# The output projection of three groups of heads put off to the last group, in a gated attention and MLP kernel

## The chip, the cores and the metric

The kernel runs on one core of a Trainium2 chip. A core has a matrix engine (TensorE, "PE" in the profile, with its weight loads listed apart as "PEld"), a vector engine (VectorE, "DVE"), an activation engine (ScalarE, "ACT"), a general engine (GpSimd, "POOL") and a queue engine that issues transfers (SyncE, "SP"). Each engine takes its instructions in the order of its own queue, and waits for other engines through semaphores. TensorE writes its results to PSUM, which has eight banks of 128 partitions by 512 floats; everything else lies in SBUF or in the chip's main memory.

The metric is the time of one execution on the device in microseconds (us), lower is better. Three runs of the kernel before took 1194.57, 1199.56 and 1199.92 us; the median is 1199.56 us.

## The reference

Everything is computed for 2048 tokens of width 448, in float32:

```python
x = A_x                                        # 2048 x 448
g = sigmoid((x * gate_w).sum(-1))              # one gate per token
q, k, v = split(x @ wqkv)                      # 16 heads of 28
p = softmax(q @ k.T * 28 ** -0.5)              # per head, 2048 x 2048
a = concat_heads(p @ v) @ wo                   # the output projection
y = (x - mean(x)) / sqrt(var(x) + 1e-5)        # layer norm
b = gelu(y @ w1 + b1) @ w2 + b2                # width 1792 inside
out = g * a + (1 - g) * b
```

Products on TensorE are made in a rounded float32 format. To keep the precision, a factor is split into a high and a low part, and a product is three products: high by high, high by low, low by high.

## The kernel before, in words

The tokens are cut into four chunks of 512 (`NC`, `CH`), each of four tiles of 128 tokens (`TPC`). The 16 heads are cut into four groups of four (`NG`); a head takes 32 of the 128 partitions.

**Stage 1, projections of x.** For each chunk `c` seven tiles of q and k (`qk_tile(c, m)`, line 156, eleven products each) and four tiles of v (`v_tile`, line 170) are made. Between them stands the preparation of the layer norm: `ln_stats` (line 189) loads two tiles of x (`bxr`) and takes mean and variance on VectorE; `ln_rows` (line 196) makes the reciprocal deviation; `ln_turn` (line 202) turns means and deviations into rows with two transposes on TensorE (line 207), into two parts of one bank. VectorE copies each result out (line 208) and SP stores it. `ln_load` (line 105) brings the rows back, repeated over all partitions, as `lnr`; `ln_apply` (line 108) loads a tile of x and normalizes it on GpSimd and ScalarE for the MLP. TensorE goes through its instructions in the order of the program text; for the other engines a planner sets the order in this stage and the next.

**Stage 2, the MLP.** Two layers of products (`mlp1`, line 430, and `mlp2`, line 445) for one chunk after the other. The result `b` without its bias goes to main memory (`gbs`). Products for the row maxima of the scores are filled in between (`Filler`, `RowMax`, line 308, each followed by a VectorE maximum, lines 288 and 290).

**Stage 3, attention.** The order of all engines is written out by hand. The loop at line 637 runs over units; a unit is one head's scores of 128 keys by 512 queries, and an iteration takes five units (`U`). There are 205 iterations for four groups by four chunks by 16 key tiles by four heads. In each iteration `scores` (line 587) issues

- up to three products for row maxima (`filler.max.issue`): one into bank 5, later one into bank 6, later one into bank 5 again,
- 15 score products into banks 0 to 4 (line 596), and two exponentials on ScalarE (line 601), one over three banks and one over two;

then `pv_mm` (line 622) adds to the outcome of the chunk in bank 7: eight products in most iterations, sixteen in some (four iterations hold five steps of four products).

When a group and chunk are done, the generator `finish` (line 518) is started, and one of its steps is run behind each of the iterations named in `STEPS` (2, 5, 7, 8, 9, 10 after the end): bank 7 is copied out as `ob`; the sums of the softmax are inverted and spread through main memory (`lt`, `rls`, `rc`); GpSimd scales `ob` and splits it into `oh` and `ol` (lines 534 to 536); and in four further steps `project` (line 508) multiplies one tile of 128 tokens by this group's part of `wo`: three products (lines 511 to 513) into a bank which `take` (line 500) hands out as 6, 5, 6, 5 in turn, and a VectorE operation (line 514) that adds the product times the gate to `acc`. `acc` holds all 16 tiles in SBUF through the whole stage. In group 0 `load_acc` (line 569) fills it with `gbs` for one chunk at step 6, and `gate_acc` (line 572) adds the bias `b2b` and multiplies by one minus the gate, in eight GpSimd instructions for each chunk at step 14. So `project` is called 64 times, 16 times for each group; in the last group the result is stored to `out`. For the very last chunk `finish_last` (line 543) does the same without the way through main memory.

The row maxima of the next chunk are stored by GpSimd's queue (`ms<-mt`, line 278) and loaded by SP at step 12 (`load_qm`, line 411). They are ended at iteration 188.

Of the kernel before, what the change touches and what calls it, by code (L numbers as in the profile page):

```python
# [15 lines left out]
P = 128  # L16
S = 2048
# [22 lines left out]
def kernel(ctx: ExitStack, tc: tile.TileContext, xt, wqk, wv, wo, xk, w1, b1, w2, b2,  # L40
# [43 lines left out]
    def staged(width):  # L84
        return my.tile([P, CH], F32, name="r", bufs=3)[:, :width]
# [19 lines left out]
    def ln_load(c):  # L105
        nc.sync.dma_start(lnr, lns.rearrange("(n t) i -> n (t i)", n=2)[:, c * CH:(c + 1) * CH].partition_broadcast(P))

    def ln_apply(c, t):
        x = staged(CH)
        nc.sync.dma_start(x, xt[t, :, c * CH:(c + 1) * CH])  # L110
        nc.gpsimd.tensor_sub(x, x, lnr[:, 0])
        nc.gpsimd.tensor_mul(x, x, lnr[:, 1])
        nc.scalar.activation(yh[:, t], x, AF.Copy)
        if t < 3:
            nc.gpsimd.tensor_sub(yl[:, t], x, yh[:, t].bitcast(F32))
        else:
            nc.gpsimd.tensor_sub(yh[64:128, t], x[64:128], yh[64:128, t].bitcast(F32))


    with tc.tile_pool(name="qx", bufs=2) as qx, tc.tile_pool(name="qo", bufs=3) as qo, \  # L120
# [93 lines left out]
        for c in range(NC):  # L214
            for m in range(NM):
# [243 lines left out]
    for c in range(NC):  # L459
# [21 lines left out]
        for i in range(TPC):  # L481
            if c + 1 < NC:
                ln_apply(c + 1, i)
            mlp2(c, i)
# [12 lines left out]

    spare = 0

    def take():  # L500

        nonlocal spare
        spare += 1
        return bank[:, 5 + spare % 2]

    acc = aw.tile([P, NT, D], F32, name="acc")
    b2b = aw.tile([P, D], F32, name="b2b")
    def project(g, tt, oh, ol):

        po = take()[:, :D]  # L510
        nc.tensor.matmul(po, oh, woh[:, g], start=True, stop=False)  # L511
        nc.tensor.matmul(po, oh, wol[:, g], start=False, stop=False)  # L512
        nc.tensor.matmul(po, ol, woh[:, g], start=False, stop=True)  # L513
        nc.vector.scalar_tensor_tensor(acc[:, tt], po, gate[:, tt:tt + 1], acc[:, tt], op0=OP.mult, op1=OP.add)  # L514
        if g == NG - 1:
            nc.sync.dma_start(out[tt], acc[:, tt])

    def finish(g, c, pv):
# [12 lines left out]
        yield True  # L531
        oh = ao.tile([P, CH], F32R, name="oh")
        ol = ao.tile([P, CH], F32R, name="ol")
        nc.gpsimd.tensor_mul(ob, ob, rc)
        nc.gpsimd.tensor_copy(oh, ob)
        nc.gpsimd.tensor_sub(ol, ob, oh.bitcast(F32))
        yield True
# [5 lines left out]
    def finish_last(g, c, pv):  # L543

        ob = ao.tile([P, CH], F32, name="ob")
        rc = ao.tile([P, CH], F32, name="rc")
        oh = ao.tile([P, CH], F32R, name="oh")
        ol = ao.tile([P, CH], F32R, name="ol")
        psl = bank[:, 0]
        tiles = [slice(i * P, (i + 1) * P) for i in range(TPC)]  # L550
        for sl in tiles:
            nc.scalar.activation(ob[:, sl], pv[:, sl], AF.Copy)
        for sl in tiles:
            nc.tensor.matmul(psl[:, sl], sel, ob[:, sl], start=True, stop=True)
        for i, sl in enumerate(tiles):
            nc.vector.reciprocal(rc[:, sl], psl[:, sl])
            nc.vector.tensor_mul(ob[:, sl], ob[:, sl], rc[:, sl])
# [11 lines left out]
    def load_acc(c):  # L569
        nc.sync.dma_start(acc[:, c * TPC:(c + 1) * TPC], gbs[c * TPC:(c + 1) * TPC].rearrange("t p d -> p t d"))  # L570

    def gate_acc(c):
        for tt in range(c * TPC, (c + 1) * TPC):
            nc.gpsimd.tensor_add(acc[:, tt], acc[:, tt], b2b)
            nc.gpsimd.tensor_scalar(acc[:, tt], acc[:, tt], ngate[:, tt:tt + 1], None, op0=OP.mult)

# [54 lines left out]
    with tc.manual_schedule(engines={E.SP, E.Pool, E.Activation, E.DVE}):  # L631
# [5 lines left out]
        for u in range(0, 4 * steps, U):  # L637
            units = list(range(u, min(u + U, 4 * steps)))
            while at < units[-1] // 4:
# [3 lines left out]
                if n == 0:  # L643
# [35 lines left out]
        while summed < steps:  # L679
            pv_mm(summed)  # L680
            summed += 1
        finish_last(NG - 1, NC - 1, pv)

# [52 lines left out]
```

## Time and profile before

| | |
|---|---|
| median of three runs | 1199.56 us |
| the profiled execution's own time | 1192.24 us |
| its span from first to last instruction | 1190.5 us |
| mean granted TensorE clock | 0.987 |
| busy: TensorE, VectorE, ScalarE, GpSimd | 95%, 64%, 53%, 28% |
| stage 1 about | 0 to 130 us |
| stage 2 about | 130 to 490 us |
| stage 3 about | 490 to 1190 us |

The views used below: the list of groups of instructions gives for each line, engine and shape the total busy time, the mean in ns, and the idle time of the engine before them with what ended it. The list of waits gives engine and line, what it waited for, the total in us, how often, and the longest. The timeline gives start and duration in us, the engine, the line, the operation, and in brackets the idle time just before. A row of the timeline that ends in x2 stands for two instructions in a row. The stage table gives for each stretch of time the busy time of each engine and the granted TensorE clock as a share of full speed. The chain is the sequence of work that led to the last instruction.

### The profile page before, as it was taken

To read this page: it belongs to the slowest core of one execution; us is meant where nothing else is said; L and a number is where in the kernel's file an instruction comes from. 1 tells how busy PE (TensorE), PEld (TensorE's weight loads), DVE (VectorE), ACT (ScalarE), POOL (GpSimd) and SP (SyncE) were. 2 spreads that over 40 slices of the span, in tenths; PEclk is the share of its full clock that TensorE was granted. 3 is DMA by queue.
4 is the path that set the end of the run, shared out by engine and by line. 5 is a ranking of instruction groups with operands and counts; after the bars stand their busy time and mean duration, and the time that the engine had idled before them with its cause. 6 is when DMAs were issued, how large, how long until landed. Compare 5 with 4: busy or idle time off the path is not lost.

```text
span 1190.5 us, 19884 instructions
## 1 busy us (share of the span) xinstructions
PE 1134.6 (95%) x8136; PEld 679.7 (57%) x8136; DVE 764.2 (64%) x1081; ACT 636.0 (53%) x668; POOL 330.0 (28%) x355
## 2 busy tenths in 40 slices
PE   6989989999999999999999999999999999999997
PEld 5777757777777777644444444444444444444443
DVE  3442198888878888566666666666666666666403
ACT  5333461132131140376767766766766776777774
POOL 4051368045133131136136211301301211220220
PEclk9998999999999999899999999999999999999998
DMA  8886742002101032362200220100210100001101
GB/s 273 255 255 235 210 139 87 16 9 77 39 16 33 17 87 60 102 158 84 58 17 19 57 60 11 35 17 10 66 53 17 28 26 25 11 11 48 34 26 55
DMA packets 53519, 84.35 MB, mean 71 GB/s; under 512 B 8676, under 2 KB 28660, under 8 KB 52628
## 3 DMA queue, kind: packets, MB, share of 16 engines
q1 hardware_dynamic: 49236, 76.96, 21.6%
q0 software_dynamic: 4192, 6.12, 2.2%
q8 instruction: 64, 1.05, 0.4%
q14 instruction: 27, 0.22, 0.1%
HBM read 56.40 MB, written 26.49 MB: 70 GB/s over the span
## 4 chain that ended last, share of the span: by engine, by line
PE 83%; DMA 6%; DVE 4%; POOL 3%; issue 1%; ACT 1%; SPq 0%; DVEq 0%; POOLq 0%; ACTq 0%
PE bank L625 20%; PE bank L596 18%; PE bank L308 14%; PE bank L438 10%; PE bank L450 4%; PE bank L453 4%; PE bank L451 4%; PE bank L163 3%; PE bank L511 2%; DVE acc L514 2%; DMA r<-in_w 2%; DMA xraw<-in_xt 1%; PE bank L179 1%; PE bank L513 1%; PE bank L512 1%
## 5 line engine op out<-in xcount | busy, mean ns | idle before, releaser
L601 ACT ACTIVATE pt<-bank 128x1536 f32<-128x1536 f32 (+1 forms) x410 | 484.6, 1234 | 197.8 <-PE bank L596 193.0
L288 DVE TENSOR_REDUCE mx<-bank 128x1 f32<-128x512 f32 x624 | 412.6, 686 | 145.5 <-PE bank L308 135.3
L625 PE MATMUL bank<-pt,vg 128*32 128x512 f32 x2048 | 262.8, 604 | 0.0
L308 PE MATMUL bank<-khi,qd 28*128 28x512 f32 x512 | 241.8, 478 | 21.7 <-DVE acc L514 20.8
L290 DVE TENSOR_REDUCE mx<-bank 128x2 f32<-128x1024 f32 x200 | 235.2, 1218 | 37.7 <-PE bank L308 37.6
L596 PE MATMUL bank<-qh,klo 28*128 28x512 f32 x1024 | 185.3, 397 | 0.0
L308 PEld LDWEIGHTS bank<-khi,qd 28*128 28x128 f32 x512 | 92.3, 181 | 152.9 <-DVE mx L288 80.1
L596 PE MATMUL bank<-qh,khi 29*128 29x512 f32 x768 | 164.4, 477 | 0.3 <-ACT h L456 0.3
L438 PE MATMUL bank<-y,w1f 128*128 128x512 f32 x616 | 153.1, 399 | 1.1 <-ACT h L442 1.1
L596 PE MATMUL bank<-ql,khi 28*128 28x512 f32 x768 | 136.4, 392 | 0.0
L438 PEld LDWEIGHTS bank<-y,w1f 128*128 128x128 f32 x616 | 112.9, 188 | 37.0 <-issue 12.4
L443 POOL TENSOR_TENSOR hl<-h,hh 128x512 fp32r<-128x512 f32 x56 | 72.2, 1289 | 171.2 <-ACT h L442 160.0
L514 DVE SCALAR_TENSOR_TENSOR acc<-bank,gate,acc 128x448 f32<-128x448 f32 x64 | 43.7, 684 | 105.3 <-PE bank L513 104.1
L596 PEld LDWEIGHTS bank<-qh,klo 28*128 28x128 f32 x1024 | 92.2, 186 | 5.0
L524 POOL DMA_DIRECT2D lt<-ob x15 | 10.8, 720 | 301.6 <-DVE ob L523 301.6
L625 PEld LDWEIGHTS bank<-pt,vg 128*32 128x32 f32 x2048 | 45.7, 108 | 84.2 <-issue 83.0
L308 PE MATMUL bank<-khr,qd 28*128 28x512 f32 x512 | 81.8, 467 | 7.0 <-DVE mx L290 4.7
L453 PE MATMUL bank<-w2h,hl 128*128 128x448 f32 x224 | 84.6, 378 | 0.0
L450 PE MATMUL bank<-w2h,hh 128*128 128x448 f32 x224 | 84.5, 377 | 0.0
L596 PEld LDWEIGHTS bank<-qh,khi 29*128 29x128 f32 x768 | 65.9, 183 | 31.9 <-ACT pt L601 26.4
L456 ACT ACTIVATE h<-bank 128x448 f32<-128x448 f32 x16 | 8.7, 543 | 139.2 <-PE bank L453 139.2
L451 PE MATMUL bank<-w2l,hh 128*128 128x448 f32 x224 | 82.2, 367 | 0.0
(97 smaller groups left out, 1285.3 us busy)
## 6 DMA issues: line engine op xcount, KB each, us to landing
qk<-hl SPq DMA_DIRECT2D x28, 512.0 KB
xraw<-in_xt SPq DMA_DIRECT2D x16, 256.0 KB
vs<-vt SPq DMA_DIRECT2D x16, 256.0 KB
r<-in_xt SPq DMA_DIRECT2D x16, 256.0 KB
rc<-rls POOLq DMA_DIRECT2D x60, 64.0 KB, 2.2
bxr<-in_xk SPq DMA_DIRECT2D x8, 448.0 KB
r<-in_w SPq DMA_DIRECT2D x14, 256.0 KB
gbs<-h SPq DMA_DIRECT2D x16, 224.0 KB
```

Of the source, the lines that this page charges most:

```text
L288: nc.vector.reduce_max(self.mx[:, c0:c0 + 1], bank[:, b0], axis=AX)
L290: nc.vector.reduce_max(self.mx[:, c0:c1 + 1:c1 - c0], bank[:, b0:b1 + 1], axis=AX)
L308: nc.tensor.matmul(bank[:, b], self.qds[self.n][r, i * P:(i + 1) * P], khi[self.n // NC][r, k * 512:(k + 1) * 512], start=True, stop=True)
L438: nc.tensor.matmul(ps, a, b, start=(i == 0), stop=(i == len(ops) - 1))
L443: nc.gpsimd.tensor_sub(hl[f], h, hh[f].bitcast(F32))
L450: nc.tensor.matmul(a, hh[f][:, sl], w2h[f], start=(f == 0), stop=False)
L451: nc.tensor.matmul(a, hh[f][:, sl], w2l[f], start=False, stop=False)
L453: nc.tensor.matmul(a, hl[f][:, sl], w2h[f], start=False, stop=(f == NF - 1))
L514: nc.vector.scalar_tensor_tensor(acc[:, tt], po, gate[:, tt:tt + 1], acc[:, tt], op0=OP.mult, op1=OP.add)
L596: nc.tensor.matmul(bank[:, u % U], a[r, k * P:(k + 1) * P], b[r], start=(i == 0), stop=(i == 2))
L601: nc.scalar.activation(t, bank[:, b:b + len(units)], AF.Exp, scale=SCALE)
L625: nc.tensor.matmul(pv[32 * j:32 * j + 32, :], vg[n // NC][:, k, 32 * j:32 * j + 32], probs.pop(4 * step + j), start=(k == 0), stop=(k == N ...
```

## The change

The change has three parts.

1. **Projection.** `finish` of groups 0 to 2 no longer projects. GpSimd writes the scaled, split outcome into tiles that stay in SBUF (`outcome`, three groups by two parts by 2048 tokens). In the last group each token tile gets one projection of twelve products, three for each group, into one bank, which is always bank 6, and one VectorE operation `gated` in place of four. `finish_last` puts the nine products of groups 0 to 2 of its first tile ahead of the sums of the softmax and those of the other three tiles behind them, in four different banks (1 to 4).
2. **`acc`.** The tile `acc` of 16 token tiles is gone. `load_acc` and `gate_acc` run in the last group (steps 6 and 10) and use the buffers of `vg` and `klo`, which are free by then.
3. **Layer norm preparation.** `ln_apply` is split in two: `ln_fetch` issues the load of x, `ln_apply` computes. In stage 1 the rows of the first four tiles are turned after tile `m` = 5 of chunk 1 (before: 2), and those of the other twelve after tile 4 of chunk 3 (before: tile 5 of chunk 2). `ln_load` moves from tile 3 to tile 6 of chunk 1; the four `ln_apply` calls move from chunks 1 and 2 to chunks 2 and 3.

```diff
+    def ln_fetch(c, t):
+        lnx[c, t] = staged(CH)
+        nc.sync.dma_start(lnx[c, t], xt[t, :, c * CH:(c + 1) * CH])
+
     def ln_apply(c, t):
-        x = staged(CH)
-        nc.sync.dma_start(x, xt[t, :, c * CH:(c + 1) * CH])
+        x = lnx.pop((c, t))
...
-                if c == 1 and m in (0, 2, 3):
-                    (ln_rows if m == 0 else ln_turn if m == 2 else lambda a, b: ln_load(0))(0, TPC)
+                if c == 1 and m == 1:
+                    ln_rows(0, TPC)
+                if c == 1 and m == 5:
+                    ln_turn(0, TPC)
+                if c == 1 and m == 6:
+                    ln_load(0)
...
-                if c == 2 and m in (3, 5):
-                    (ln_rows if m == 3 else ln_turn)(TPC, NT)
-                if c == 1 and m in (4, 6) or c == 2 and m in (0, 2):
-                    ln_apply(0, m // 2 - 2 if c == 1 else m // 2 + 2)
+                if c == 2 and m in (0, 1, 2, 4):
+                    ln_fetch(0, (0, 1, 2, 2, 3)[m])
+                if c == 2 and 3 <= m < 6 or c == 3 and m == 0:
+                    ln_apply(0, m - 3 if c == 2 else 3)
+                if c == 2 and m == 6:
+                    ln_rows(TPC, NT)
+                if c == 3 and m == 4:
+                    ln_turn(TPC, NT)
...
-    def project(g, tt, oh, ol):
-
-        po = take()[:, :D]
-        nc.tensor.matmul(po, oh, woh[:, g], start=True, stop=False)
-        nc.tensor.matmul(po, oh, wol[:, g], start=False, stop=False)
-        nc.tensor.matmul(po, ol, woh[:, g], start=False, stop=True)
-        nc.vector.scalar_tensor_tensor(acc[:, tt], po, gate[:, tt:tt + 1], acc[:, tt], op0=OP.mult, op1=OP.add)
-        if g == NG - 1:
-            nc.sync.dma_start(out[tt], acc[:, tt])
+    outcome = [[aw.tile([P, S], F32R, name=f"o{x}{g}") for x in "hl"] for g in range(NG - 1)]
+    acc = {}
+
+    def project(c, i, oh, ol, po, groups):
+
+        sl = slice(i * P, (i + 1) * P)
+        for g in groups:
+            if g < NG - 1:
+                h, l = (x[:, c * CH:(c + 1) * CH][:, sl] for x in outcome[g])
+            else:
+                h, l = oh[:, sl], ol[:, sl]
+            nc.tensor.matmul(po, h, woh[:, g], start=(g == 0), stop=False)
+            nc.tensor.matmul(po, h, wol[:, g], start=False, stop=False)
+            nc.tensor.matmul(po, l, woh[:, g], start=False, stop=(g == NG - 1))
+
+    def gated(c, i, po):
+        tt = c * TPC + i
+        a = acc[c][:, i]
+        nc.vector.scalar_tensor_tensor(a, po, gate[:, tt:tt + 1], a, op0=OP.mult, op1=OP.add)
+        nc.sync.dma_start(out[tt], a)
...
+        if g < NG - 1:
+            return
         yield True
         for i in range(TPC):
-            sl = slice(i * P, (i + 1) * P)
-            project(g, c * TPC + i, oh[:, sl], ol[:, sl])
+            po = bank[:, 6, :D]
+            project(c, i, oh, ol, po, range(NG))
+            gated(c, i, po)
             yield True
...
+        po = [bank[:, 1 + i, :D] for i in range(TPC)]
         for sl in tiles:
             nc.scalar.activation(ob[:, sl], pv[:, sl], AF.Copy)
+        project(c, 0, oh, ol, po[0], range(NG - 1))
         for sl in tiles:
             nc.tensor.matmul(psl[:, sl], sel, ob[:, sl], start=True, stop=True)
+        for i in range(1, TPC):
+            project(c, i, oh, ol, po[i], range(NG - 1))
...
-        for i, sl in enumerate(tiles):
-            project(g, c * TPC + i, oh[:, sl], ol[:, sl])
+        for i in range(TPC):
+            project(c, i, oh, ol, po[i], [NG - 1])
+            gated(c, i, po[i])
...
-                if g == 0:
+                if g == NG - 1:
                     if k == 6:
                         load_acc(c)
-                    if k == 14:
+                    if k == 10:
                         gate_acc(c)
```

More of the change, by code (lines that the diff above doesn't have):

```diff
@@ L482 @@
             if c + 1 < NC:
+                ln_fetch(c + 1, i)
                 ln_apply(c + 1, i)
@@ L496 @@
     wol = aw.tile([P, NG, D], F32R, name="wol")
[L498 to L506, printed above, removed]
-    b2b = aw.tile([P, D], F32, name="b2b")
-    def project(g, tt, oh, ol):
-        po = take()[:, :D]
[L511 to L514, printed above, removed]
-        if g == NG - 1:
-            nc.sync.dma_start(out[tt], acc[:, tt])
+    b2b = aw.tile([P, D], F32, name="b2b")
+    outcome = [[aw.tile([P, S], F32R, name=f"o{x}{g}") for x in "hl"] for g in range(NG - 1)]
[15 more added lines that the diff above has]
+        nc.sync.dma_start(out[tt], a)
     def finish(g, c, pv):
@@ L531, in finish @@
         yield True
-        oh = ao.tile([P, CH], F32R, name="oh")
-        ol = ao.tile([P, CH], F32R, name="ol")
+        if g < NG - 1:
+            oh, ol = (x[:, c * CH:(c + 1) * CH] for x in outcome[g])
+        else:
+            oh, ol = ao.tile([P, CH], F32R, name="oh", bufs=1), ao.tile([P, CH], F32R, name="ol", bufs=1)
         nc.gpsimd.tensor_mul(ob, ob, rc)
@@ L569, in load_acc @@
     def load_acc(c):
-        nc.sync.dma_start(acc[:, c * TPC:(c + 1) * TPC], gbs[c * TPC:(c + 1) * TPC].rearrange("t p d -> p t d"))
+        a = aq.tile([P, NT, P], F32, name="vg", bufs=2) if c % 2 == 0 else aq.tile([P, S], F32, name="klo", bufs=2)
+        if c % 2 == 0:
+            a = a.rearrange("p a b -> p (a b)")
+        acc[c] = a[:, :TPC * D].rearrange("p (t d) -> p t d", d=D)
+        nc.sync.dma_start(acc[c], gbs[c * TPC:(c + 1) * TPC].rearrange("t p d -> p t d"))
     def gate_acc(c):
-        for tt in range(c * TPC, (c + 1) * TPC):
-            nc.gpsimd.tensor_add(acc[:, tt], acc[:, tt], b2b)
-            nc.gpsimd.tensor_scalar(acc[:, tt], acc[:, tt], ngate[:, tt:tt + 1], None, op0=OP.mult)
+        for i in range(TPC):
+            a, tt = acc[c][:, i], c * TPC + i
+            nc.gpsimd.tensor_add(a, a, b2b)
+            nc.gpsimd.tensor_scalar(a, a, ngate[:, tt:tt + 1], None, op0=OP.mult)
     tc.keep_in_program_order(nc.scalar.activation(gate, zall, AF.Exp, scale=-1.0))
```

10 lines of the change are left out of this document (6 added, 4 removed).

## The prediction, made before the changed kernel ran

> **What bounds the kernel now.** I read the page's sums first, then the list of waits of TensorE by stage, then the timeline of ScalarE in stage 3, whose exponentials mark every iteration. Page:
>
> ```profile
> span 1190.5 us, 19884 instructions
> PE 1134.6 (95%) x8136; PEld 679.7 (57%) x8136; DVE 764.2 (64%) x1081; ACT 636.0 (53%) x668; POOL 330.0 (28%) x355
> ```
>
> TensorE is the bound as a whole, so what counts is its products and its own waits. Its waits in 500 to 1020 us, then in 1020 to 1191 us, then in 0 to 135 us:
>
> ```profile
> PE bank L308 <- DVE acc L514: 17.7, 22, 0.8
> ...
> PE bank L308 <- DVE acc L514: 3.1, 4, 0.8
> ...
> PE bank L207 <- DVE rows L208: 8.3, 2, 5.5
> ```
>
> In attention nearly every idle moment of TensorE is one and the same: the next row maximum product (bank 5) waits until VectorE has read a projection out of bank 5. In stage 1 the second of two transposes waits for VectorE to copy out the first. Timeline of ScalarE, first a finish of group 0, then the last one of group 2:
>
> ```profile
> 588.25 2.37 ACT L601 ACTIVATE pt<-bank 128x1536 f32<-128x1536 f32 x2 [1.20 <-PE bank L596]
> 590.95 2.37 ACT L601 ACTIVATE pt<-bank 128x1536 f32<-128x1536 f32 x2 [0.33 <-PE bank L596]
> 593.66 2.37 ACT L601 ACTIVATE pt<-bank 128x1536 f32<-128x1536 f32 x2 [0.34 <-PE bank L596]
> 596.37 2.37 ACT L601 ACTIVATE pt<-bank 128x1536 f32<-128x1536 f32 x2 [0.34 <-PE bank L596]
> 599.91 2.37 ACT L601 ACTIVATE pt<-bank 128x1536 f32<-128x1536 f32 x2 [1.18 <-PE bank L596]
> 603.42 2.37 ACT L601 ACTIVATE pt<-bank 128x1536 f32<-128x1536 f32 x2 [1.14 <-PE bank L596]
> 608.01 2.37 ACT L601 ACTIVATE pt<-bank 128x1536 f32<-128x1536 f32 x2 [2.23 <-PE bank L596]
> ...
> 617.04 2.37 ACT L601 ACTIVATE pt<-bank 128x1536 f32<-128x1536 f32 x2 [2.89 <-PE bank L596]
> ...
> 1030.73 2.37 ACT L601 ACTIVATE pt<-bank 128x1536 f32<-128x1536 f32 x2 [1.20 <-PE bank L596]
> ...
> 1047.64 2.37 ACT L601 ACTIVATE pt<-bank 128x1536 f32<-128x1536 f32 x2 [2.71 <-PE bank L596]
> ```
>
> Four iterations in a row without a projection (588.25 to 599.91) take 11.66 us: three of 2.71 and one of 3.54, which has sixteen outcome products. The next four, each with one projection of three products, take 17.13 (599.91 to 617.04), and the last four of group 2 take 16.91. So a finish costs 5.47 to 5.25 us, about 5.36. Within it a projection into bank 6 lengthens its iteration by 0.80 (599.91 to 603.42, less 2.71), one into bank 5 by 1.88 (603.42 to 608.01): 1.08 more, for the wait listed above. ScalarE needs 2.37 of the 2.71, so it doesn't hold back an iteration that loses its projection; that iteration falls to 2.71, as its neighbours show.
>
> **Groups 0 to 2: projections removed.** Twelve finishes at 5.36: -64.3 us. Nothing takes their place there: the GpSimd steps that make `oh` and `ol` are the same, only their target is another tile. The 48 VectorE operations that go with them are off the path where they don't hold bank 5.
>
> **Last group: nine more products in each of twelve blocks.** The same form, 448 columns with a new weight for each product, runs in `mlp2`; timeline of TensorE:
>
> ```profile
> 187.78 0.36 PE L450 MATMUL bank<-w2h,hh 128*128 128x448 f32 x1
> ...
> 189.20 0.37 PE L451 MATMUL bank<-w2l,hh 128*128 128x448 f32 x1
> ```
>
> Seven steps in 1.42 us: 0.203 each. 12 x 9 x 0.203 = +21.9 us, all on the path.
>
> **Bank 6 for every projection.** The finish of chunk 12 still runs beside the maxima; its two projections in bank 5 lose their wait: -2.2 us (2 x 1.08); those of chunks 13 and 14 run after or at the end of the maxima and had none. Bound: nothing gained, or every one of the twelve blocks waits as a bank 5 one does now, +13.0. I take the first because the bank 6 blocks of now, with a maximum into bank 6 in the middle of each iteration, show only the 0.80. [...]
>
> **`acc` in the last group.** Eight GpSimd instructions for each chunk move; groups by shape, then GpSimd's and SP's timelines in the last chunk but one:
>
> ```profile
> L575 POOL TENSOR_SCALAR acc<-acc,ngate 128x448 f32<-128x448 f32 x16 | 22.5, 1404 | 1.6
> ...
> L574 POOL TENSOR_TENSOR acc<-acc,b2b 128x448 f32<-128x448 f32 x16 | 18.3, 1142 | 0.0
> ...
> 1113.11 1.28 POOL L536 TENSOR_TENSOR ol<-ob,oh 128x512 fp32r<-128x512 f32 x1
> 1119.56 0.60 POOL L278 DMA_DIRECT2D ms<-mt  x1 [5.17 <-DVE mt L277]
> ...
> 1121.96 0.51 SPq L416 DMA_DIRECT2D qh<-ms  x1
> ...
> 1135.45 2.37 ACT L601 ACTIVATE pt<-bank 128x1536 f32<-128x1536 f32 x2 [0.28 <-PE bank L596]
> ```
>
> Four times 1.404 + 1.142 is 10.2 us for a chunk, while GpSimd otherwise waits. In that chunk they stand ahead of the store of the row maxima (line 278): after `ol`, 1114.4, they end at 1124.6, so the store goes out 5 us later, and SP's load of it (line 416, with the `out` stores that follow it in SP's queue) as much. The scores that need it begin just before 1135.45: 13.5 us of cover today, 8 then. Cost 0; if the cover were gone, at most 5. The loads of `gbs` (four, one for each chunk, as now) go behind SP's `qh` and `ql` loads into buffers whose readers are done a chunk earlier: 0.
>
> **The end.** Timeline of TensorE, ScalarE and VectorE:
>
> ```profile
> 1173.84 2.78 PE L625 MATMUL bank<-pt,vg 128*32 128x512 f32 x24
> 1176.77 0.78 ACT L552 ACTIVATE ob<-bank 128x128 f32<-128x128 f32 x4 [1.71 <-issue]
> 1177.10 1.16 PE L554 MATMUL bank<-ob,sel 128*128 128x128 f32 x8 [0.47 <-ACT ob L552]
> ...
> 1183.20 0.29 DVE L557 TENSOR_TENSOR ob<-ob,rc 128x128 f32<-128x128 f32 x1
> ...
> 1184.75 0.57 PE L512 MATMUL bank<-wol,oh 128*128 128x448 f32 x1
> 1185.12 0.57 PE L513 MATMUL bank<-woh,ol 128*128 128x448 f32 x1
> ...
> 1186.85 0.69 DVE L514 SCALAR_TENSOR_TENSOR acc<-bank,gate,acc 128x448 f32<-128x448 f32 x1 [0.44 <-PE bank L513]
> ```
>
> The outcome products end at 1176.62. Nine products then take 1.83, to 1178.45, and the sums 1.16 more, to 1179.61 (now 1178.26), so VectorE's chain ends 1.35 later, at 1184.84. The other 27 products run beside it, 5.48, to 1185.09; the last twelve take 2.44, to 1187.53; the last VectorE operation 0.69, to 1188.22, against 1187.54 now: +0.7. Today these products go at 0.37 (1184.75 to 1185.12), for a TensorE that had idled; if that stays, 39 x 0.167 = +6.5 more.
>
> **Stage 1.** Products of one stretch, a load, the waiting transposes, what VectorE did ahead of the second copy, and the clock after each wait (chain, timelines, stage table; the seventh figure of a stage row is the granted clock):
>
> ```profile
> 42.88 4.55 DMA bxr<-in_xk
> ...
> 105.28 17.96 PE bank L163 x77
> ...
> 46.60 0.27 PE L207 MATMUL bank<-ident,mr 128*4 128x128 f32 x1
> 49.71 0.27 PE L207 MATMUL bank<-ident,mr 128*4 128x128 f32 x1 [2.83 <-DVE rows L208]
> ...
> 90.05 0.69 DVE L154 TENSOR_TENSOR xh<-xraw,xh 64x512 fp32r<-64x512 f32 x1 [1.08 <-ACT xh L150]
> ...
> 91.38 0.27 DVE L208 COPY rows<-bank 12x128 f32<-12x128 f32 x1
> ...
> 50.90:54.60 3.70, 3.70 (x11) 2.88 (x10) 0.79 (x2) 0.60 (x1) 0.00 (x0) 0.54 0.82 219
> 91.80:95.40 3.60, 3.60 (x10) 2.83 (x10) 0.88 (x2) 1.31 (x3) 2.55 (x2) 0.50 0.92 345
> ```
>
> The second turn waits 5.5 us because VectorE, in its order, first serves the x loads of chunk 3. In the built program it comes in chunk 3, where no x is loaded any more, and only the usual `hl` copy stands ahead: some 0.5 is left (two steps of 0.27), -5.0. The first turn is no better off: ahead of its copy VectorE now has the statistics of a `bxr` tile, whose load SP issues behind the store of tile 2. That tile ends at 46.6. Its store waits for VectorE, which first has the statistics of an earlier `bxr` (landed at 42.88 + 4.55 = 47.4) and two copies of x among six operations; at 0.69 each the store goes out near 52. Another 4.55 for the load, a little for the store ahead of it and two more operations put the copy near 59, an estimate from these rows. TensorE is there after three more tiles of 2.57 (17.96 over seven), at 54.3: some 4.6 of wait in place of 2.83, +1.8. Bounds: 0.5, as for the other, to 8, if two more stores go ahead. The clock cost 3.70 x 0.46 = 1.7 after the first and 1.8 after the second wait; the second goes: -1.8. Together -5.0, bounds -10 to +2. [...]
>
> **Sum.** -64.3 + 21.9 - 2.2 + 0.7 - 5.0 = -48.9 us against the profiled execution's 1192.24: 1143.3. That execution lies 7.3 below the median of the runs, 1199.56; with it the median after is 1150.6, and I predict 1150.
>
> **Rivals.**
> *The single bank waits.* All twelve blocks pay the 1.08 of today's bank 5: +13, 1163. [...] Against: an iteration lies between them, and VectorE needs 684 ns.
> *The layer norm part loses.* The first turn waits 8 or more and the clock gains nothing: 1157.
> *The long blocks are slow.* If twelve products in a row didn't overlap weight loads, each would take both of these (the rows of line 511):
>
> ```profile
> L511 PEld LDWEIGHTS bank<-woh,oh x64: 186/186/330, 558.2 to 1185.1; 128*128 128x128 f32 x64
> L511 PE MATMUL bank<-woh,oh x64: 468/470/742, 558.2 to 1185.5; 128*128 128x448 f32 x64
> ```
>
> 186 + 470 = 656 ns, which on 144 products is 144 x 0.453 = 65 us more: 1216, slower than before. It decides from 0.203 + 48.9/144 = 0.54 us per product on. Against it stand the 0.203 of `mlp2`.
>
> **How the numbers follow.** Forecast 0.66 (own range 1139 to 1158), layer norm 0.14, bank 0.13, slow blocks or something as large 0.07. The range 1138 to 1170 takes in the first three; its low end is the forecast with all of stage 1's waits gone and some of the 7.3 missing. Half a per cent (6 us) is about what a measurement can tell: faster 0.93, same 0.02, slower 0.05, from the last case.
>
> **What would show it.** Groups 0 to 2: iterations of 2.71 and 3.54 alone, and no wait of line 308's product on a gated sum. Last group: blocks of twelve at 0.203, iterations some 2.6 longer than their neighbours. Stage 1: second turn under 1 us, first at 3 to 6. Wrong if iterations without projection stay above 2.71, if the first score product after a block waits, or if TensorE waits for `qh` of the last chunk.

## The result, and the profile after

| | before | after |
|---|---|---|
| median of the runs, four of each | 1199.74 us | 1148.36 us |
| ratio to before, 95% interval | | 0.9588 [0.9549, 0.9628] |
| the profiled execution's own time | 1192.24 us | 1146.98 us |
| its span | 1190.5 us | 1145.2 us |
| mean granted TensorE clock | 0.987 | 0.991 |

The change saves 51.4 us by the medians and 45.3 us between the two profiled executions. The page of the kernel after, its sums:

```profile
span 1145.2 us, 19823 instructions
...
PE 1116.6 (98%) x8136; PEld 678.4 (59%) x8136; DVE 731.6 (64%) x1033; ACT 635.9 (56%) x668; POOL 331.0 (29%) x355
```

The number of products is the same as before, 8136. TensorE is now busy for 98% of the span, in place of 95%. Its list of waits in the kernel after, in 500 to 980 us, then 980 to 1146 us, then 0 to 135 us (waiting for what, sum, how often, longest):

```profile
PE bank L321 <- DVE mx L301: 0.2, 1, 0.2
...
PE bank L287 <- DVE mf L337: 0.6, 1, 0.6
...
PE bank L212 <- DVE rows L213: 4.0, 2, 3.6
```

The wait for a gated sum, 20.8 us in 26 places before, is gone altogether; of the 8.3 us at the two turns in stage 1, 4.0 are left. ScalarE's timeline after, first a finish of group 0, then the four long blocks of chunk 12, then the last ones of chunk 13:

```profile
587.63 2.37 ACT L634 ACTIVATE pt<-bank 128x1536 f32<-128x1536 f32 x2 [0.34 <-PE bank L629]
591.19 2.37 ACT L634 ACTIVATE pt<-bank 128x1536 f32<-128x1536 f32 x2 [1.19 <-PE bank L629]
593.90 2.37 ACT L634 ACTIVATE pt<-bank 128x1536 f32<-128x1536 f32 x2 [0.34 <-PE bank L629]
596.60 2.37 ACT L634 ACTIVATE pt<-bank 128x1536 f32<-128x1536 f32 x2 [0.33 <-PE bank L629]
...
1007.60 2.37 ACT L634 ACTIVATE pt<-bank 128x1536 f32<-128x1536 f32 x2 [0.33 <-PE bank L629]
1012.93 2.37 ACT L634 ACTIVATE pt<-bank 128x1536 f32<-128x1536 f32 x2 [2.96 <-PE bank L629]
1018.42 2.37 ACT L634 ACTIVATE pt<-bank 128x1536 f32<-128x1536 f32 x2 [3.13 <-PE bank L629]
1024.84 2.37 ACT L634 ACTIVATE pt<-bank 128x1536 f32<-128x1536 f32 x2 [4.05 <-PE bank L629]
1030.40 2.37 ACT L634 ACTIVATE pt<-bank 128x1536 f32<-128x1536 f32 x2 [3.19 <-PE bank L629]
...
1069.16 2.37 ACT L634 ACTIVATE pt<-bank 128x1536 f32<-128x1536 f32 x2 [3.70 <-PE bank L629]
1074.37 2.37 ACT L634 ACTIVATE pt<-bank 128x1536 f32<-128x1536 f32 x2 [2.84 <-PE bank L629]
1079.60 2.36 ACT L634 ACTIVATE pt<-bank 128x1536 f32<-128x1536 f32 x2 [2.86 <-PE bank L629]
```

In group 0 an iteration takes 3.56 (587.63 to 591.19, sixteen outcome products) or 2.70, whether a finish runs or not. A block of twelve takes 5.2 when no maxima run beside it (1069.16 to 1074.37, 1074.37 to 1079.60). The chunk 12 blocks, beside the maxima, take 5.33 and then 5.49 and 5.56, and 6.42 where sixteen outcome products fall in. Timeline after of several engines: the two turns with what went ahead of the first, the start of stage 3, the GpSimd steps of the last chunk but one, a block, and the tail:

```profile
51.50 1.18 SPq L196 DMA_DIRECT2D bxr<-in_xk  x1
...
57.35 1.15 DVE L198 BATCH_NORM_STATS2 st<-bxr 128x6 f32<-128x448 f32 x2 [0.98 <-DMA bxr<-in_xk]
...
58.64 0.25 DVE L213 COPY rows<-bank 4x128 f32<-4x128 f32 x1
...
58.94 0.37 PE L212 MATMUL bank<-ident,mr 128*4 128x128 f32 x1 [3.65 <-DVE rows L213]
...
112.47 0.28 PE L212 MATMUL bank<-ident,mr 128*12 128x128 f32 x1 [0.37 <-DVE rows L213]
...
486.47 0.49 PE L629 MATMUL bank<-qh,khi 29*128 29x512 f32 x1
...
490.65 0.49 PE L321 MATMUL bank<-khr,qd 28*128 28x512 f32 x1 [2.00 <-DVE mx L301]
...
493.47 0.79 PE L321 MATMUL bank<-khr,qd 28*128 28x512 f32 x1 [1.01 <-DVE mx L301]
...
1063.14 1.40 POOL L608 TENSOR_SCALAR vg<-vg,ngate 128x448 f32<-128x448 f32 x1
...
1064.49 0.64 POOL L291 DMA_DIRECT2D ms<-mt  x1
...
1066.75 0.51 SPq L429 DMA_DIRECT2D qh<-ms  x1
...
1076.20 0.37 PE L526 MATMUL bank<-wol,oh 128*128 128x448 f32 x1
...
1078.23 0.36 PE L527 MATMUL bank<-woh,ol 128*128 128x448 f32 x1
...
1129.66 1.04 PE L658 MATMUL bank<-pt,vg 128*32 128x512 f32 x8
...
1139.75 2.51 DVE L532 SCALAR_TENSOR_TENSOR klo<-bank,gate,klo 128x448 f32<-128x448 f32 x4 [0.94 <-PE bank L527]
...
1141.17 0.36 PE L527 MATMUL bank<-woh,ol 128*128 128x448 f32 x1
```

From the second to the twelfth product of a block (1076.20 to 1078.23) ten steps take 2.03, so 0.203 each. In the tail the outcome products end at 1130.70 and the last gated sum at 1142.26.

Where the time went is easiest to see in stages. The borders are worked out from the trace: the first score product, then the first score product of iterations 10, 160 and 204. The twelve finishes of groups 0 to 2 end at iteration 164, so eleven of them lie in the third row.

| stretch | before | after | difference | the prediction's terms |
|---|---|---|---|---|
| to the first score product | 490.52 | 486.47 | -4.05 | -5.0 |
| iterations 0 to 9 | 33.66 | 35.52 | +1.86 | 0 |
| iterations 10 to 159 | 501.92 | 442.95 | -58.97 | 11 x -5.36 = -58.96 |
| iterations 160 to 203 | 145.96 | 161.17 | +15.21 | -5.36 + 21.9 - 2.2 = +14.3 |
| iteration 204 to the end | 18.41 | 19.08 | +0.67 | +0.7 |
| sum | | | -45.28 | -48.9 |

Two rows are as forecast to 0.03 us; that the third one is, is in part luck, as the section on the prediction shows. The other three miss by 3.7 us in sum; experiments 1 and 5 to 9 are about those.

### The profile page after: what moved, and what is told of

Its sections match the earlier page's. It is cut to its first block, busy times and chain, and to the rows that moved or that the text cites. A ratio compares the mean times of both kernels' runs of the same rounds, so it can differ in the third digit from the quotient of the medians.

```text
span 1145.2 us, 19823 instructions
## 1 busy us (share of the span) xinstructions
PE 1116.6 (98%) x8136; PEld 678.4 (59%) x8136; DVE 731.6 (64%) x1033; ACT 635.9 (56%) x668; POOL 331.0 (29%) x355
## 4 chain that ended last, share of the span: by engine, by line
PE 89%; DMA 4%; POOL 3%; DVE 2%; issue 1%; ACT 1%; SPq 0%; POOLq 0%; ACTq 0%; DVEq 0%
PE bank L658 22%; PE bank L629 20%; PE bank L321 15%; PE bank L451 10%; PE bank L168 4%; PE bank L466 4%; PE bank L463 4%; PE bank L464 4%; PE bank L184 2%; PE bank L525 1%; DMA bxr<-in_xk 1%; PE bank L526 1%; PE bank L527 1%; DMA xraw<-in_xt 1%; POOL hl L456 1%
## 5 line engine op out<-in xcount | busy, mean ns | idle before, releaser
L629 PE MATMUL bank<-qh,klo 28*128 28x512 f32 x1024 | 179.0, 395 | 0.0
L629 PE MATMUL bank<-qh,khi 29*128 29x512 f32 x768 | 161.8, 484 | 0.3 <-ACT h L469 0.3
L629 PE MATMUL bank<-ql,khi 28*128 28x512 f32 x768 | 133.6, 393 | 0.0
L629 PEld LDWEIGHTS bank<-qh,khi 29*128 29x128 f32 x768 | 63.3, 183 | 36.8 <-ACT pt L634 32.1
L454 ACT ACTIVATE hh<-bank,b1s 128x512 fp32r<-128x512 f32 x56 | 38.4, 685 | 81.9 <-PE bank L451 81.8
```

The costliest lines, as they stand in the source:

```text
L629: nc.tensor.matmul(bank[:, u % U], a[r, k * P:(k + 1) * P], b[r], start=(i == 0), stop=(i == 2))
```

## The experiments

The theory (A) is the prediction's sum: a bank that the maxima use next makes them wait, the products removed give back their whole time, the block of twelve costs its products. Rivals are that a single bank waits, that the layer norm part loses, and that long blocks stall something. Times are medians; "before" on the same chip was 1198.2 us for experiments 1 to 4 and 1198.35 us for 5 to 8.

**1. Bank 6 alone, in the kernel before.**

```diff
-        return bank[:, 5 + spare % 2]
+        return bank[:, 6]
```

> The kernel before, with every projection in bank 6 and nothing else changed. Theory A (the prediction's terms: only the bank that the next row maximum product uses waits): in each of the twelve finishes of groups 0 to 2 and in that of chunk 12 two blocks lose 1.08 us, 26 x 1.08 = 28 us less, about 1172, and the wait of line 308's product on a gated sum is gone. Rival B (the single bank waits: each projection follows the last into the same bank): the wait moves to the projection or stays with the maximum product in bank 6; no gain, 1200, up to 26 us more.

Measured: 1183.88 us, ratio 0.9886 [0.9852, 0.9919], by the ratio 13.7 us less (9.7 to 17.7): half of what theory A said. In its trace iterations 10 to 159 are 15.67 us shorter than before, 1.42 for each of eleven finishes and not 2.16; iterations 160 to 203 are 2.72 shorter. The list of waits of TensorE in 500 to 1020 us, and ScalarE's timeline in the same finish as the prediction shows for before:

```profile
PE bank L308 <- DVE mx L288: 2.6, 3, 2.0
```

```profile
605.62 2.37 ACT L601 ACTIVATE pt<-bank 128x1536 f32<-128x1536 f32 x2 [1.19 <-PE bank L596]
609.12 2.37 ACT L601 ACTIVATE pt<-bank 128x1536 f32<-128x1536 f32 x2 [1.13 <-PE bank L596]
612.79 2.37 ACT L601 ACTIVATE pt<-bank 128x1536 f32<-128x1536 f32 x2 [1.30 <-PE bank L596]
```

The wait on the gated sum is gone, as A has it. The first block still takes 3.50 (605.62 to 609.12). But the second takes 3.67, where its 4.59 less 1.08 would give 3.51. So 0.16 comes back in each block that follows another one, and some 0.2 in the iteration after the last. Rival B falls as a whole, and theory A misses a small term. Experiment 9 names it.

**2. The projections of groups 0 to 2 left out, in the kernel before.**

```diff
         nc.gpsimd.tensor_sub(ol, ob, oh.bitcast(F32))
+        if g < NG - 1:
+            return
         yield True
```

> The kernel before, with the projections of groups 0 to 2 left out (48 calls; the scaled outcome is still computed, the output lacks these groups). Theory A: twelve finishes at 5.36 us, 64.3 less, about 1135, and every iteration of these groups at 2.71 or 3.54. Rival (work in the shadow of something else, ScalarE's 2.37 or VectorE): part of it doesn't come back, 1145 or more.

Measured: 1138.16 us, ratio 0.9495 [0.9465, 0.9525], 60 us less (57 to 64). In the trace iterations 10 to 159 take 444.57, 57.35 less than before, and 160 to 203 take 140.59, 5.37 less: together 62.7 of the 64.3. What is missing is two iterations, number 16 and 67 counted from 0, that are 0.94 and 0.75 us longer there than in the kernel after. Number 16 comes before the first projection; what it waits for has to do with `acc`, and is told in the section on the prediction. Number 67 takes from 2.70 to 3.74 us in the eleven traces, whatever the kernel. The iterations that lose a projection fall by the same 58.4 us in both kernels. So nothing stands in for the products that are gone: the first term holds.

**3. The layer norm part alone, in the kernel before.**

```diff
+    def ln_fetch(c, t):
+        lnx[c, t] = staged(CH)
+        nc.sync.dma_start(lnx[c, t], xt[t, :, c * CH:(c + 1) * CH])
...
-                if c == 1 and m in (0, 2, 3):
-                    (ln_rows if m == 0 else ln_turn if m == 2 else lambda a, b: ln_load(0))(0, TPC)
+                if c == 1 and m == 1:
+                    ln_rows(0, TPC)
+                if c == 1 and m == 5:
+                    ln_turn(0, TPC)
...
-                if c == 2 and m in (3, 5):
-                    (ln_rows if m == 3 else ln_turn)(TPC, NT)
...
+                if c == 3 and m == 4:
+                    ln_turn(TPC, NT)
```

> The kernel before, with the layer norm part of the change alone. Theory A: the prediction's sum for it, 5.0 us less (second turn 5.0, its clock 1.8, first turn 1.8 more), 1195. From the trace of after, where the v products of chunk 3 end 3.1 us earlier than before and the first score product comes 4.05 us earlier but meets a longer stretch at half clock: 3 less, 1197. Rival C (the part loses): 1200 or more.

Measured: 1188.63 us, ratio 0.9933 [0.9907, 0.9959], 8.0 us less (4.9 to 11.1). In its trace the two turns wait 3.4 us, in place of 8.3 before. Rival C falls. The 5.0 of theory A lies at the low end of the interval.

**4. The nine products left out, in the kernel after.**

```diff
-            nc.tensor.matmul(po, h, woh[:, g], start=(g == 0), stop=False)
+            nc.tensor.matmul(po, h, woh[:, g], start=(g == first), stop=False)
...
-            project(c, i, oh, ol, po, range(NG))
+            project(c, i, oh, ol, po, [NG - 1], NG - 1)
```

> The kernel after, with the nine products of groups 0 to 2 left out in the twelve blocks of chunks 12 to 14 (the output of these chunks lacks three groups; the last chunk is as it is). Theory A: 12 x 9 x 0.203 = 21.9 us less, 1126.5. The trace of after has 2.6 to 2.9 us more in a block's iteration than in its neighbours, where a block of three took 0.80: 1.8 to 2.1 per block, 22 to 25 us. Rival (the long block itself stalls something, the four of chunk 12 above all): 28 us or more, below 1120.

Measured: 1124.23 us, ratio 0.9387 [0.9353, 0.942]: 24 us less than after, by the two ratios; their intervals leave some 5 us either way, so the trace decides. There iterations 160 to 203 take 139.37 in place of 161.17, 21.80 less. That is the 108 products at 0.203 (21.9) and nothing else, so the excess of chunk 12's blocks is not a matter of their length: a block of three has it too (3.51 for the first, then 3.67).

**5. The layer norm part put back, in the kernel after.** The reverse of experiment 3, of which this is the core:

```diff
-                if c == 1 and m == 5:
-                    ln_turn(0, TPC)
...
-                if c == 3 and m == 4:
-                    ln_turn(TPC, NT)
+                if c == 1 and m in (0, 2, 3):
+                    (ln_rows if m == 0 else ln_turn if m == 2 else lambda a, b: ln_load(0))(0, TPC)
...
+                if c == 2 and m in (3, 5):
+                    (ln_rows if m == 3 else ln_turn)(TPC, NT)
```

> The kernel after, with the layer norm part put back as it was before. Theory A (the prediction's term): 5.0 us more than after, 1153. By the first run of this part alone (ratio 0.9933 to before) it is 8 us, 1156. By the trace of after, where the first score product comes 4.05 us earlier than before and 1.9 are lost again in the first ten iterations at half clock, it is 2 to 4, 1151. If the two parts were not independent (a rival), below 1149 or above 1160.

Measured: 1155.78 us, ratio 0.9651 [0.9628, 0.9675], 7.4 us more than after (2 to 13 by the two intervals). So the part is worth 7.4 and 8.0 us by the medians in the two kernels. Nothing speaks against the two parts of the change adding up, but the intervals are too wide to show it to better than 5 us. Both figures are more than the 4.05 - 1.86 = 2.2 us that the two profiled executions differ by in the stretches it touches. The first score product tells why. In the four traces with the old order it stands at 490.52 (before), 495.43, 494.30 and 495.53 us (experiments 1, 2, 5). In the five with the new order and the same transposes it stands at 486.47 (after), 487.91, 483.87, 487.75 and 487.31 (experiments 3, 4, 6, 9). The means are 493.9 and 486.7, 7.3 apart. The profiled execution of before was an early one: at the start of iteration 10 it stands at 524.2 us, the three others of the old order at 531.5 to 532.1. The traces show most of what makes up the 7.3. The two turns wait 8.3 (before) and 9.4 to 10.5 us (the others) in the old order, and 2.1 to 4.4 in the new. And TensorE has 13.7 (before) and 17.1 us (the others) at half clock ahead of the first score product in the old order, 10.2 to 13.7 in the new.

**6. Banks 6 and 5 in turn, in the kernel after.**

```diff
-            po = bank[:, 6, :D]
+            po = bank[:, 6 - i % 2, :D]
```

> The kernel after, with the projections of the last group in banks 6, 5, 6, 5 as before. Theory A: only chunk 12 runs beside the maxima; its two blocks in bank 5 wait 1.08 each, 2.2 us more, 1150.5. After the run of the kernel before with bank 6 alone, where a finish fell by 1.42 us and not by 2.16 (each block behind another in bank 6 paid 0.17 more, the iteration behind the last 0.23): 1.4 more, 1149.8, and in the trace the five iterations from the first block of chunk 12 on are 1.4 longer in sum. [...]

Measured: 1151.96 us, ratio 0.9612 [0.9586, 0.9637], against 0.9588 [0.9549, 0.9628]: the times alone don't tell the two apart. The trace does. The five iterations from the first block of chunk 12 on take 5.352 + 6.410 + 6.217 + 6.468 + 2.705 = 27.15 us, against 25.73 in after: 1.43 more, as expected from experiment 1. TensorE's list of waits, 980 to 1050 us of this kernel:

```profile
PE bank L321 <- DVE vg L532: 1.7, 2, 0.8
```

Two waits of a row maximum product for a gated sum are back. That the blocks of chunks 13 and 14, with no maxima beside them, lose as well is not shown: the span is 4.7 us longer than in after (1149.9 and 1145.2), of which 1.28 stand ahead of the first score product and 1.43 in these five iterations, and the half clock at the start of stage 3 lasts 17.0 us, in place of 10.2.

**7. The two transposes of a turn in two banks, in the kernel after.**

```diff
-            ps = next_ps()
             for n in range(2):
+                ps = next_ps()
```

> The kernel after, with the two transposes of each turn in two banks in place of two parts of one. If the wait of the second transpose is for the bank that VectorE reads the first from (theory A), 3.65 + 0.35 us of wait go and with them the 1.7 us of half clock behind the first: 4 to 6 less, 1142.5 to 1144.5. Rival: TensorE waits next for something else in stage 1 (a weight or x load), or the stretch at half clock comes elsewhere: less than 2, 1146.5 or more.

Measured: 1145.29 us, ratio 0.9556 [0.953, 0.9581], 3.1 us less than after; its slowest run (1145.94) is below the fastest of after (1146.98). That is less than the 4 to 6 of theory A and more than the 2 of its rival. The second transposes follow the first by 0.11 us (56.86 and 56.97; 108.46 and 108.57), so the wait was for the shared bank. The last v product begins 3.92 us earlier (122.56), but the first score product comes only 2.35 earlier. TensorE's list of waits in 0 to 135 us of this kernel:

```profile
PE bank L451 <- ACT h L455: 2.0, 1, 2.0
...
PE bank L451 <- DVE zall L187: 0.9, 1, 0.9
```

These two waits at the start of the MLP, 2.9 us, do not stand in the same list of after: TensorE now waits there for ScalarE and VectorE. What is late next can so take a part of the gain. How much of the 1.6 us that were lost between the last v product and the first score product these two took is not shown, since the other waits in the MLP differ between the two as well.

**8. Beside that, the start of stage 3.**

```diff
-    nc.vector.tensor_scalar_add(gate, gate, 1.0)
-    nc.vector.reciprocal(gate, gate)
-    nc.vector.tensor_scalar(ngate, gate, -1.0, 1.0, op0=OP.mult, op1=OP.add)
...
-                    if 2 <= k < 6:
-                        load_wo(k - 2)
+                    if k in (5, 7, 9, 11):
+                        split_wo((k - 5) // 2)
+                    if k in (1, 3, 5, 7):
+                        fetch_wo((k - 1) // 2)
+                    if k == 12:
+                        nc.vector.tensor_scalar_add(gate, gate, 1.0)
+                        nc.vector.reciprocal(gate, gate)
+                        nc.vector.tensor_scalar(ngate, gate, -1.0, 1.0, op0=OP.mult, op1=OP.add)
```

> As the one before, and at the start of stage 3 the gate's three VectorE operations and the four copies of wo moved behind the first maxima (copies two key tiles behind their loads, the gate at key tile 12). If the 5.41 + 4.72 us of iterations 1 and 2, against 2.70 each, come from VectorE being held by the gate and by loads of wo (waits of line 321's product of 2.0 and 1.0) and from the half clock that follows, 3 to 4.7 less than the one before: 1138 to 1141. If the half clock comes from something else, only the waits, 1 to 3, 1141 to 1143.

Measured: 1141.93 us, ratio 0.9538 [0.9515, 0.9562], 6.4 us less than after; its slowest run (1144.02) is below the fastest of after. Against experiment 7 it is 3.4 us less by the medians, but the two intervals overlap. Of the two cases that were expected it lies in the first by its difference and in the second by its time, so the times don't choose between them. Iterations 0 to 9 take 31.19 us, 4.6 less than in experiment 7 (35.80) and 4.3 less than in after. ScalarE's timeline at the start of stage 3, after and then this kernel:

```profile
491.67 2.37 ACT L634 ACTIVATE pt<-bank 128x1536 f32<-128x1536 f32 x2 [0.72 <-PE bank L629]
497.76 2.37 ACT L634 ACTIVATE pt<-bank 128x1536 f32<-128x1536 f32 x2 [3.72 <-PE bank L629]
```

```profile
487.88 2.37 ACT L635 ACTIVATE pt<-bank 128x1536 f32<-128x1536 f32 x2 [0.16 <-PE bank L630]
491.91 2.37 ACT L635 ACTIVATE pt<-bank 128x1536 f32<-128x1536 f32 x2 [1.66 <-PE bank L630]
494.83 2.37 ACT L635 ACTIVATE pt<-bank 128x1536 f32<-128x1536 f32 x2 [0.56 <-PE bank L630]
```

The iteration of 6.09 us (491.67 to 497.76) has no counterpart; the longest is 4.03. VectorE no longer stands still for the gate and the loads of `wo` while maxima wait behind them: line 321's waits there are 1.2 us, in place of 3.2 in experiment 7. TensorE has one stretch of 3.4 us at half clock (the seventh figure of a stage row is the granted clock), in place of 10.2:

```profile
489.06:492.47 3.41, 3.41 (x25) 1.90 (x18) 1.39 (x3) 1.75 (x3) 0.00 (x0) 0.50 0.63 166
```

That the waits are shorter is shown. That the half clock goes with them is not: this execution was the fastest of five, with a mean clock of 0.997, and the other four have 0.992 to 0.995, as the runs of experiment 7 have. This is the fastest kernel here.

**9. Two maxima in the iterations behind a block, in the kernel after.**

```diff
-            scores(units, min(3, filler.due()))
+            busy = u // 4 // NT // NC == NG - 1 and fin is not None and 7 <= since <= 10
+            scores(units, min(2 if busy else 3, filler.due()))
```

> The kernel after, with two row maximum products in place of three in the iterations that follow a block (the maxima left over come later). In after the five iterations from the first block of chunk 12 on take 5.323 + 5.487 + 6.420 + 5.560 + 2.937 = 25.73 us, 0.8 more than the prediction's 0.80 + 1.83 for each block. If that is the third product, which goes into bank 5 and finds VectorE late with the first one because the gated sum stands ahead of it (theory), the second to fifth iteration fall by 0.17 to 0.23 each and by the little that a product costs: the sum is 24.7 to 25.0, and nothing is left behind the last block (2.7). If it is the product in the middle, which goes into bank 6 and has to wait for the gated sum itself (rival), the sum stays at 25.5 or more. The whole time can't tell: the maxima left over cost something later.

One execution was taken. ScalarE's timeline in chunk 12's blocks, and then the wait that leads TensorE's list in 1055 to 1090 us:

```profile
1011.99 2.37 ACT L634 ACTIVATE pt<-bank 128x1536 f32<-128x1536 f32 x2 [0.32 <-PE bank L629]
1017.33 2.37 ACT L634 ACTIVATE pt<-bank 128x1536 f32<-128x1536 f32 x2 [2.97 <-PE bank L629]
1022.55 2.37 ACT L634 ACTIVATE pt<-bank 128x1536 f32<-128x1536 f32 x2 [2.85 <-PE bank L629]
1028.64 2.37 ACT L634 ACTIVATE pt<-bank 128x1536 f32<-128x1536 f32 x2 [3.72 <-PE bank L629]
1033.86 2.37 ACT L634 ACTIVATE pt<-bank 128x1536 f32<-128x1536 f32 x2 [2.85 <-PE bank L629]
```

```profile
PE bank L321 <- DVE mx L301: 4.9, 6, 0.9
```

The blocks are down to 5.34, 5.22, 6.09, 5.22, and the five iterations to 5.330 + 5.213 + 6.087 + 5.220 + 2.598 = 24.45 us, even below the range expected (0.12 comes back in the iteration after these five, 2.82 for 2.70): the excess is the third maximum product. Its weight load in the kernel after says the same, from the timelines of VectorE and of the weight loads:

```profile
1011.96 0.68 DVE L532 SCALAR_TENSOR_TENSOR vg<-bank,gate,vg 128x448 f32<-128x448 f32 x1 [2.80 <-PE bank L527]
...
1013.30 0.18 PEld L321 LDWEIGHTS bank<-khi,qd 28*128 28x128 f32 x1 [0.21 <-DVE mx L301]
```

It goes into bank 5 and finds VectorE still reading the first one, because the gated sum of 0.68 us stands ahead of that. The rival, the product in bank 6, is excluded: it still runs, and the second block takes 5.21, no more than a block beside which no maxima run (1069.16 to 1074.37 in after). The whole, at 1163.5 us, is slower all the same. The nine maxima left over are issued in one go in iteration 187. Six of them wait for VectorE, 4.9 us in sum, ScalarE gets no scores for 14.2 us, and the granted clock is at 0.50 from 1070 to 1080 us (a maximum product takes 0.79 us at 1071.24, 0.50 at 1067.12). Iterations 187 and 188 take 15.92 + 9.63 us in place of 6.18 + 6.07, 13.3 more.

## Why the prediction was right, and where not

The median, 1148.36 us, lies 1.6 below the 1150 that was forecast and within the likeliest case's own range. The large steps were right in mechanism and size; that the whole came so near is in part luck, since misses offset each other. The steps one by one:

- **Groups 0 to 2, -64.3: right.** The iterations stand at 2.70 and 3.56, as the neighbours without projection had shown. Taken one by one, the 44 iterations that lose a projection in the stretch with eleven finishes fall by 58.40 us, 5.2 to 5.46 a finish, where the term says 58.96. The whole stretch fell by 58.97; that this agrees to 0.01 is luck, since 1.16 us come from `acc` (below) and the other iterations lose 0.60 again. Experiment 2 took 62.7 us out of the two stretches with the same products.
- **Nine more products in twelve blocks, +21.9: right.** 0.203 a product in the trace, 21.80 us by experiment 4. The rival of slow blocks (0.54 a product or more) is excluded.
- **Bank 6, -2.2: mis-sized by some 0.8.** The step that failed is "the bank 6 blocks of now, with a maximum into bank 6 in the middle of each iteration, show only the 0.80". In before such a block is the first of its finish, or follows one in bank 5, whose 1.08 us of wait give VectorE time to catch up. With bank 6 every time, the second block pays 0.16, and the third, the fourth and the iteration behind the last 0.23 each (25.73 us for five iterations in after). Experiment 9 shows that the third maximum causes it. One bank is still the better choice for these blocks: banks 6 and 5 in turn take 1.43 us more in experiment 6, since a row maximum product takes the next bank. For the transposes of experiment 7 two banks are better: their waits of 3.65 and 0.37 us are gone.
- **`acc` and GpSimd in the last chunk but one, 0: right.** The last multiplication ends at 1064.5, then the store goes out, and SP's load at 1066.75. The scores that need it begin at 1081.1, and TensorE doesn't wait. The cover was 14.4 us and not the 8 of the prediction. The store did go out 5.7 us behind the end of the maxima (1058.8), where before it followed by 0.3 (1119.3 and 1119.56); but the five iterations up to those scores are 7.3 us longer, because of the blocks of twelve, and the prediction left that out.
- **`acc` out of group 0, put at 0: it gained some 1 us.** The prediction asked what the loads of `gbs` cost in the last group and not what they cost in group 0, where they go. In before SP issues the load of 896 KB for chunk 1 at 535.45, GpSimd the 8 KB of `lt` at 537.09. These land 6.1 us later, where the median is 2.3. VectorE waits for them, and the maxima behind it with TensorE's next product (0.70) wait too. Iteration 16, in which this falls, takes 4.69 to 4.93 us in the four kernels that load `acc` in group 0 (before and experiments 1 to 3), and 3.76 to 3.77 in the seven others. No projection has run by then, and experiments 3 and 5 exclude the layer norm part. That the larger load holds up the smaller one is argued from these rows. VectorE's row in before and in after:

```profile
543.20 0.25 DVE L526 RECIPROCAL lt<-lt 128x16 f32<-128x16 f32 x1 [1.75 <-DMA lt<-ob]
...
539.27 0.25 DVE L543 RECIPROCAL lt<-lt 128x16 f32<-128x16 f32 x1
```

- **The end, +0.7: right.** From the end of the outcome products to the last gated sum it takes 11.56 us (1130.70 to 1142.26), against 10.92 before, +0.64. The 39 products run at 0.20; the surcharge of 6.5 us for an engine that had idled didn't come. TensorE no longer idles there, and the granted clock is 1.00 (1130 to 1143 us), where it was 0.50 in before (1180.9 to 1190).
- **Stage 1, -5.0: right in mechanism, probably too small.** The second turn fell to 0.37 (forecast 0.5), the first rose to 3.65 (forecast 4.6), by the chain forecast: a `bxr` load issued at 51.50, its statistics from 57.35 on, the copy at 58.64. The last v product began 5.4 us earlier (126.48, before 131.90). Of this, 1.4 went until the first score product; one more stretch of 3.4 us at half clock, at 160.9, costs 1.7. Another 1.86 went in iterations 0 to 9, so that 2.2 were left between the two profiled executions. Those ten iterations take 33.7 to 38.7 us in the ten traces other than experiment 8's, so the 1.86 lies within what differs from execution to execution. By experiments 3 and 5 the part is worth 7.4 to 8.0 us over the runs, with intervals from 2 to 13. The term was sized on one execution whose turns waited 8.3 us, where the three others waited 9.4 to 10.5.
- **The 7.3 us between the profiled execution and the median: wrong.** The prediction carried them over to the kernel after as a constant. There the gap is only 1.4 (1148.36 - 1146.98). The profiled execution of before was ahead of the three other traces of the same order by 3.8 to 5.0 us at the first score product and by 7.3 to 7.9 at iteration 10, about the whole offset. The sum was 3.7 too good (1143.3 for 1146.98) and the offset 5.9 too large; they cancelled but for 2.2 us, 1.6 after 1150.6 was rounded to 1150. That is luck.

What isn't settled is why one order of work varies by 4 to 5 us up to the first score product from execution to execution. Between before and the three others, 1.1 to 2.2 us are the waits at the turns and 1.7 is one stretch more at half clock; why those differ stays open.

## What to carry to other kernels

Price a wait by its iteration: two neighbours of the same form, one with and one without, gave a sum of 58.96 us for the 58.40 that the iterations concerned lost. But when a wait goes, look at what had caught up during it: here VectorE stayed late, and the next product paid 0.16 to 0.23 us a block. When work moves, ask also what it held up at its old place (here some 1 us in group 0). A sum made against one profiled execution holds for that execution; its distance from the median (7.3 us here, 1.4 in the kernel after) doesn't carry over to the next kernel.

## What the runs showed of the hardware

In all eleven traces the half clock comes in stretches of 3.4 us or a multiple of it (3.4, 6.8, 10.2, 13.7, 17.1), the ones at the very end aside. In some TensorE was busy all through (3.40 of 3.40 us at 160.90 in after). Stage tables of the kernel after and, last, of before (length, busy time of PE, PEld, VectorE, ScalarE, GpSimd, then the granted clock):

```profile
160.90:164.30 3.40, 3.40 (x10) 2.61 (x9) 2.99 (x4) 2.54 (x5) 1.80 (x2) 0.50 0.53 147
492.00:502.30 10.30, 9.29 (x52) 3.83 (x51) 5.74 (x10) 4.40 (x4) 3.39 (x3) 0.50 0.59 164
495.43:502.26 6.83, 6.83 (x45) 3.30 (x42) 3.42 (x6) 2.37 (x2) 2.27 (x2) 0.50 0.62 163
```

```profile
494.80:501.70 6.90, 6.71 (x38) 3.39 (x41) 3.23 (x6) 2.56 (x3) 2.26 (x2) 0.51 0.58 167
```

At the start of stage 3 of after TensorE waits 2.0 us, until 490.65, and 1.0 us, until 493.47, and is at half clock from 492.0 for three such stretches (10.3 us, some 5 us lost). In before it is two. The third stretch alone costs half its 3.4 us, 1.7 of the 1.86 lost there. In the ten traces other than experiment 8's, the half clock there lasts from 6.8 to 17.1 us, and iterations 0 to 9 take from 33.7 to 38.7.

TensorE was busy by the profile through both the second and the third of these stretches (495.43 to 502.26, 6.83 of 6.83 us), at a granted clock of 0.50. The longest wait in the list ahead of the three is 2.0 us. Ahead of the stretch at half clock that begins at 51.1 us in before it was the first turn's 2.83. In after, the first turn's 3.65 us of wait have a stretch of 3.4 us at their end (from 58.5), and the second's 0.37 have none (1.00 from 111 to 120 us). What sets a stretch off and what ends it is not shown.
